# Attention and SwiGLU on one core: high parts of the up weights at 192 modulo 256 bytes, low parts at 64, one order of products for all chunks

## The chip, the cores and the metric

One core of a Trainium2 chip runs the whole program. The metric is the device time of one execution in microseconds, taken as the median of several. Engines are named as the profile names them: PE is TensorE's matmul (PEld its weight load), DVE is VectorE, ACT is ScalarE, POOL is GpSimd, SP is SyncE, whose queue starts most DMAs.

## The reference

Block-causal attention and, on its output, a feed-forward layer with a gate. q, k and v are float32, the three weights float64.

```python
B, H, S, D = 8, 8, 576, 64                     # blocks of 64 positions
scores = q @ k.T / sqrt(D), masked where block_i < block_j
attn_out = softmax(scores) @ v
x = attn_out.transpose(0, 2, 1, 3).reshape(4608, 512)
g = x @ w_gate                                 # 512 x 1536
out = (g * sigmoid(g) * (x @ w_val)) @ w_out   # 1536 x 512
```

## The kernel before

**Products.** PE multiplies in float32r, which keeps fewer bits than float32. So each operand is split into a high part, rounded by ACT, and a low part, the rest, made by DVE; a product of two such operands is three matmuls: high by high, high by low, low by high. A matmul has a standing operand (the weights of the array, 128 columns, loaded ahead of it by PEld while the matmul before still runs) and a moving operand that streams past, here 256 columns of 4 bytes.

**The up weights.** w_gate and w_val are kept in SBUF as high (x = 0) and low (x = 1) tiles, made by `weight`: w_gate's odd chunks of 128 columns in `g_odd0` and `g_odd1`, its even chunks in `g_even0` and `g_even1`, w_val's chunks in `v_all0` and `v_all1` (lines 227 to 230). `w_at(which, x, i)` (line 231) gives chunk i of either matrix and either part. The pool hands out bytes in the order in which the tiles are asked for. In the program as built, before the change, the six tiles start at these bytes of a partition: g_odd0 1984, g_odd1 14272, v_all0 26560, v_all1 51136, g_even0 75712, g_even1 88064. Modulo 256 that is 192 for all of them but g_even1, which stands at 0, because g_even0 was given 16 more elements. Chunks of 512 bytes inside a tile keep the number. x's parts (`xhl`, and the tiles that take their place later) all stand at 0 modulo 256.

**Stages.** (1) Attention for 8 batches, with POOL for maxima and sums over partitions. (2) Between its products stand those of the feed-forward tiles of 256 tokens: `up` (matmuls at L1270, weights standing, x moving), then tanh on ACT and two products on DVE, then the down products (L1381 to L1383). (3) The last 1536 tokens go in three wide tiles of 512, by a scheme with 7 block products in place of 8. There `Pair.product` (L1717) takes w_gate's and w_val's own chunks for the products named 1 to 4, and sums of chunks for 5, 6 and 7, which come by DMA from `mix_d` into a ring of buffers in `sc`. High and low part of the ring's buffers both stand at 64 modulo 256, by an offset of 16 elements (`shifted`). (4) The last stage makes the output of the wide tiles and of the last narrow tiles (`product_of`, L2033). In it w_out's blocks, which by then lie in the places of the up weights, are the *moving* operand, and the hidden values stand; their high and low parts are all at 0 modulo 256.

**The order.** Every piece of work is a task with an engine, a rank, buffers and what it waits for. `in_order` plays the engines through with estimated costs and writes down one order, which is then issued, so the order on each engine is fixed before the kernel runs. The up products of a chunk are one task of 12 matmuls (four blocks d, three matmuls each); for the first two tiles they are four tasks of 3. Each task's list of matmuls is written in `products`:

```python
three = [[(lo, d, 0), (hi, d, 0), (hi, d, 1)] for d in ds]
if which or y:
    three = [[b, c, a] for a, b, c in three]
elif len(ds) > 1:
    three = [[a for a, b, c in three]] + [[b, c] for a, b, c in three]
```

So w_val's chunks and w_gate's odd ones go high, high, low for each d; w_gate's even chunks begin with the four low parts and go on with the eight high ones. `Pair.on_pe` asks for the same of the gate's products 1 and 2 in the wide tiles (`low_first`).

Of the kernel before, what the change touches and what calls it, by code (L numbers as in the profile page):

```python
# [7 lines left out]
F32 = mybir.dt.float32  # L8
F32R = mybir.dt.float32r
# [9 lines left out]
def kernel(  # L19
# [20 lines left out]
    DFF = w_gate.shape[1]  # L40
    P = 128
# [6 lines left out]
    NDC = DM // P  # L48
# [48 lines left out]
    const = ctx.enter_context(tc.tile_pool(name="const", bufs=1))  # L97
# [79 lines left out]
    def add(engine, cost, rank, fn, after=(), bufs=(), port=False, mode="", stage=""):  # L177


        bufs = [*dict.fromkeys([*bufs, *(p for u in bufs for p in getattr(u, "under", ()))])]  # L180
        t = Task(engine, cost, rank, fn, after, bufs, port, mode)
        for a in after:
            if a is not None:
                a.next.append(t)
                t.waits += 1
        for u in bufs:
            u.left += 1
        t.n, t.stage = len(tasks), stage
        tasks.append(t)
        return t  # L190


    def act_us(n, psum=False, more=0.0):
        return (0.05 if psum else 0.093) + n * 0.000833 + more

    def dve_us(n, one=False):
        return 0.07 + n * (0.00052 if one else 0.00104)

    def up_us(n):
        return n * 0.1134 + (0.012 if n < 3 * NDC else 0.0)  # L200
# [24 lines left out]


    half_w, whole_w = [P, NDC, DFF // 2], [P, NDC, DFF]
    g_odd = [const.tile(half_w, F32R, name=f"g_odd{x}") for x in range(2)]
    v_all = [const.tile(whole_w, F32R, name=f"v_all{x}") for x in range(2)]
    g_even = [const.tile([P, NDC * DFF // 2 + 16 * (1 - x)], F32R, name=f"g_even{x}") for x in range(2)]  # L230

    def w_at(which, x, i):

        if which:
            return v_all[x][:, :, i * P : (i + 1) * P]
        if i % 2:
            return g_odd[x][:, :, i // 2 * P : (i // 2 + 1) * P]
        every = g_even[x][:, 0 : NDC * DFF // 2].rearrange("p (c f) -> p c f", c=NDC)
        return every[:, :, i // 2 * P : (i // 2 + 1) * P]
# [987 lines left out]
    def feed_forward(j, t0, w, xs):  # L1227
# [19 lines left out]
        def rank(i):  # L1247
            return (10.0 + (t0 + w * i / NFC) / S) if j > 1 else SIDE[j] + w * i / NFC / S

        def up(i, which, prev):  # L1250

            ps = Buf("gv")
            ts = up_done[0]
            for y in range(2):

                chunk = []
                for ds in [range(NDC)] if j >= WHOLE else [[d] for d in range(NDC)]:

                    def products(ds=ds, y=y):
                        hi, lo = (w_at(which, k, i + y) for k in range(2))  # L1260
                        o = ps[0][:, y * w : (y + 1) * w]
                        three = [[(lo, d, 0), (hi, d, 0), (hi, d, 1)] for d in ds]
                        if which or y:
                            three = [[b, c, a] for a, b, c in three]
                        elif len(ds) > 1:
                            three = [[a for a, b, c in three]] + [[b, c] for a, b, c in three]
                        for n, (part, d, x) in enumerate(sum(three, [])):
                            first = n == 0 and 0 in ds
                            last = n == 3 * len(ds) - 1 and NDC - 1 in ds
                            nc.tensor.matmul(  # L1270
                                o, lhsT=part[:, d], rhs=xs[d][1][x][:, 0:w], start=first, stop=last
                            )

                    ts = add(
                        "PE",
                        up_us(3 * len(ds)),
                        rank(i),
                        products,
                        [ts, *(xs[d][0] for d in ds), w_done[i + y, which]],
                        [ps, *(xs[d][1] for d in ds)],  # L1280
                        stage="up",
                    )
                    ts.prev = prev
                    ts.chunk, ts.ds = chunk, ds
                    ts.even = len(ds) > 1 and not (which or y)
                    prev = ts if j >= FINE else None
                last_use.setdefault((which, i + y), []).append(ts)
            chain["up"] = up_done[0] = ts
            return ps, ts

        for i in range(0, NFC, 2):
# [37 lines left out]
            a = add("ACT", act_us(n, True), E, tanh, [tg], [pg, t])  # L1329
            a = add("DVE", dve_us(n), E, silu2, [a], [pg, t])  # L1330
            a = add("DVE", dve_us(n), E, gated, [a, tv], [pv, t, hh] if put_off else [pv, t])
            if put_off:
                u, x = divmod(j - normal + 2 * DEFER, 2)
# [12 lines left out]
            a = add("ACT", act_us(n, to is pv), E, high, [a], [to, hh])  # L1346
            a = add("DVE", dve_us(n), E, low, [a], [to, hh], to is t)
# [126 lines left out]
    def wide_tiles(mixed):  # L1474
# [189 lines left out]
        def on_pe(*args, after=(), **more):  # L1664
            line[0] = add("PE", *args[:3], [*after, line[0]], args[3], **more)
            return line[0]
# [17 lines left out]
        class Pair:  # L1684
# [42 lines left out]
            def on_pe(self, names):  # L1727
                bufs, after = [*dict.fromkeys(self.ps[SPOT[n][0]] for n in names)], []
                for name in names:
                    bufs += [self.xs[XN[name], c] for c in range(2)]  # L1730
                    after += [self.ready[XN[name], c] for c in range(2)]
                    if name in self.ring:
                        bufs.append(self.ring[name])
                        after.append(self.loads[name])
                    if name == "3":
                        after.append(kept[self.which, self.i])

                def products():
                    self.product(names, "1" in names and not self.which)

                return on_pe(up_us(6 * len(names)), self.rank, products, bufs, after=after, stage="up")

# [533 lines left out]
    with tc.manual_schedule():  # L2276
        done, shared = set(), None
        in_turn = mybir.DependencyInfo(mybir.DependencyClass.Sync, mybir.DependencyReason.DATA)
        for t in order:
# [14 lines left out]
            ds = list(t.ds)  # L2294
# [34 lines left out]
```

## Time and profile before

| what | value |
|---|---|
| median of 3 runs (lowest, highest) | 1134.91 us (1133.3, 1136.73) |
| profiled execution | 1136.55 us |
| its span, first to last instruction | 1134.7 us |
| PE, DVE, ACT, POOL busy | 98%, 85%, 54%, 27% |
| matmuls in the trace | 9612 |
| mean granted clock of TensorE | 0.997 of full speed |

The share of busy time of an engine says how much of the span it had an instruction in work. A matmul is pipelined: the next one starts long before the last one is through, so a row's time of one matmul (some 276 to 285 ns here) is its way through the array and not what it costs. What it costs is the distance from its start to the next start. For a row of several matmuls that is the start of the next row less its own start, divided by their number.

### The profile page before, as it was taken

What the parts mean: (1) busy time and instruction counts of PE and PEld (TensorE: products, weight loads), DVE (VectorE), ACT (ScalarE), POOL (GpSimd) and SP (SyncE); (2) the same over time, 40 slices, a digit from 0 to 9 for tenths busy, and PEclk for the clock granted to TensorE, in tenths of its full rate; (3) what the DMA queues carried; (4) which work ended last, traced back from release to release, by engine and by line L of the source; (5) the groups of instructions that cost most, each with busy time, mean ns of one, the idle gap of its engine ahead of it and who ended that gap; (6) DMA issues with size and microseconds to landing.
All of it is one profiled execution on the core that took longest, in us unless ns stands there. A gap on an engine that the chain in (4) does not pass through costs nothing. (4 is left out here: it accounts for less than half of the span.)

```text
span 1134.7 us, 25286 instructions
## 1 busy us (share of the span) xinstructions
PE 1114.1 (98%) x9612; PEld 1031.0 (91%) x9612; DVE 959.5 (85%) x1772; ACT 610.6 (54%) x1115; POOL 309.4 (27%) x141
## 2 busy tenths in 40 slices
PE   7999999999999999999999999999999999999998
PEld 6777888898899999999999899999999999999998
DVE  5998888677979999999998977767698887998884
ACT  6988877556555546665665555554242222454441
POOL 3113111053544264455435553553000000000000
PEclk9999999999999999999999999999999999999999
DMA  7877666576656767887877654337788976554442
GB/s 205 209 210 202 188 194 218 148 203 195 160 150 211 182 184 202 232 216 192 214 202 199 166 145 119 92 119 220 207 272 242 294 235 216 166 158 146 126 149 75
DMA packets 332617, 211.66 MB, mean 187 GB/s; under 512 B 194192, under 2 KB 290976, under 8 KB 332496
## 3 DMA queue, kind: packets, MB, share of 16 engines
q1 hardware_dynamic: 331264, 209.39, 64.3%
q8 instruction: 75, 1.23, 0.5%
q10 hardware_dynamic: 1232, 0.66, 0.2%
q14 instruction: 46, 0.38, 0.1%
HBM read 157.29 MB, written 52.69 MB: 185 GB/s over the span
## 5 line engine op out<-in xcount | busy, mean ns | idle before, releaser
L1028 POOL PARTITION_ALL_REDUCE mx<-mx x48 | 173.2, 3640 | 204.7 <-DVE mx L823 78.1
L1270 PE MATMUL gv<-xhl,v_all 128*128 128x256 f32 x1728 | 218.7, 279 | 0.6 <-DVE hhl L1317 0.6
L1270 PEld LDWEIGHTS gv<-xhl,v_all 128*128 128x128 f32 x1728 | 208.0, 188 | 4.3 <-issue 1.0
L827 POOL PARTITION_ALL_REDUCE mx<-mx x80 | 134.5, 1718 | 268.6 <-DVE wo L1127 46.0
L853 DVE TENSOR_TENSOR sc<-sc,mx 128x640 f32<-128x640 f32 (+5 forms) x168 | 127.0, 805 | 13.1 <-POOL mx L827 12.8
L1270 PE MATMUL gv<-xhl,g_even 128*128 128x256 f32 x864 | 121.1, 285 | 3.8 <-DVE t L1310 3.4
L857 ACT ACTIVATE sc<-sc 128x1024 f32<-128x1024 f32 (+3 forms) x104 | 105.0, 1029 | 33.6 <-DVE sc L853 32.8
L1270 PEld LDWEIGHTS gv<-xhl,g_even 128*128 128x128 f32 x864 | 108.9, 188 | 11.8 <-DVE t L1310 4.9
L1270 PE MATMUL gv<-xhl,g_odd 128*128 128x256 f32 x864 | 113.5, 278 | 0.0
L1270 PEld LDWEIGHTS gv<-xhl,g_odd 128*128 128x128 f32 x864 | 105.5, 188 | 2.0 <-issue 1.7
L776 ACT ACTIVATE sc<-at 128x1024 f32<-128x1024 f32 (+3 forms) x96 | 78.5, 843 | 2.7 <-DVE mx L821 1.4
L1307 ACT ACTIVATE t<-gv 128x512 f32<-128x512 f32 x72 | 43.4, 602 | 57.0 <-PE gv L1270 57.0
L750 PE MATMUL at<-parts,qk 64*128 64x320 f32 (+5 forms) x864 | 73.7, 310 | 0.0
L939 PE MATMUL at<-sc,v 128*64 128x192 f32 (+1 forms) x960 | 70.7, 302 | 0.3 <-issue 0.3
L939 PEld LDWEIGHTS at<-sc,v 128*64 128x64 f32 x960 | 61.3, 137 | 10.4 <-issue 1.8
L1768 DVE TENSOR_TENSOR sc<-sc,at 128x512 f32<-128x512 f32 x92 | 56.5, 615 | 16.5 <-ACT sc L1773 8.1
L750 PEld LDWEIGHTS at<-parts,qk 64*128 64x128 f32 x864 | 62.7, 185 | 8.4 <-issue 1.4
L1310 DVE SCALAR_TENSOR_TENSOR t<-t,gv 128x512 f32<-128x512 f32 x72 | 48.9, 680 | 23.3 <-ACT t L1307 22.9
L1381 PE MATMUL po<-wo,hhl 128*128 128x512 f32 x156 | 63.7, 409 | 0.0
L823 DVE TENSOR_TENSOR mx<-mx,sc 128x384 f32<-128x384 f32 (+2 forms) x108 | 59.0, 549 | 2.8 <-ACT sc L857 1.5
L1382 PE MATMUL po<-wo,hhl 128*128 128x512 f32 x156 | 61.3, 393 | 0.0
L1383 PE MATMUL po<-wo,hhl 128*128 128x512 f32 x156 | 60.9, 390 | 0.0
(408 smaller groups left out, 2327.4 us busy)
## 6 DMA issues: line engine op xcount, KB each, us to landing
wo<-wo_d SPq DMA_DIRECT2D x80, 512.0 KB
sc<-mix_d SPq DMA_DIRECT2D x72, 256.0 KB
h_d<-hhl SPq DMA_DIRECT2D x60, 256.0 KB
mix_d<-wo SPq DMA_DIRECT2D x48, 256.0 KB
v<-in_v_dram SPq DMA_DIRECT2D x64, 128.0 KB
mx<-h_d SPq DMA_DIRECT2D x30, 256.0 KB
parts<-h_d SPq DMA_DIRECT2D x30, 256.0 KB
qk<-in_q_dram SPq DMA_DIRECT2D x104, 72.0 KB
```

The costliest lines, as they stand in the source:

```text
L750: nc.tensor.matmul(ps[0][:, x, o : o + w], lhsT=part(1, kl)[own(x), c * P : (c + 1) * P], rhs=part(0, ql)[own(x), qs : qs + w], start=n == ...
L776: nc.scalar.mul(sc[0][:, :, o0 : o0 + gw], ps[0][:, :, 0:gw], SCALE)
L823: nc.vector.tensor_tensor(into, prev, of(c), op)
L827: nc.gpsimd.partition_all_reduce(m, m, channels=P, reduce_op=bass_isa.ReduceOp.max)
L853: nc.vector.tensor_tensor(piece(c), scores_of(c), m, ALU.subtract)
L857: nc.scalar.activation(x, x, AF.Exp)
L939: nc.tensor.matmul(third(k)[own(x), q0 - s0 :], lhsT=vt[0][:, c, own(x)], rhs=sc[0][:, x, place[c] + q0 - first[c] : place[c] + s1 - first ...
L1028: nc.gpsimd.partition_all_reduce(m, m, channels=P, reduce_op=bass_isa.ReduceOp.add)
L1270: nc.tensor.matmul(o, lhsT=part[:, d], rhs=xs[d][1][x][:, 0:w], start=first, stop=last)
L1381: nc.tensor.matmul(po, lhsT=hi, rhs=whi, start=i + y == 0, stop=False)
L1382: nc.tensor.matmul(po, lhsT=hi, rhs=wlo, start=False, stop=False)
L1383: nc.tensor.matmul(po, lhsT=lo, rhs=whi, start=False, stop=i + y == NFC - 1)
```

## The change

The six tiles are asked for in another order, with fillers between: g_odd0, v_all0, g_even0, then 128 bytes, then g_odd1, v_all1, g_even1, then 192 bytes. In the program as built they start at 1984, 14272, 38848 (all 192 modulo 256) and 51264, 63552, 88128 (all 64). Every later tile of the pool lies 256 bytes further on. And w_gate's even chunks, in the narrow and in the wide tiles, go high, high, low for each d as the others do. As the last stage reads w_out's blocks from the same places, its moving operand now steps between 192 and 64 too, except in the product named 3, of which both parts lie in g_even0.

```diff
     half_w, whole_w = [P, NDC, DFF // 2], [P, NDC, DFF]
-    g_odd = [const.tile(half_w, F32R, name=f"g_odd{x}") for x in range(2)]
-    v_all = [const.tile(whole_w, F32R, name=f"v_all{x}") for x in range(2)]
-    g_even = [const.tile([P, NDC * DFF // 2 + 16 * (1 - x)], F32R, name=f"g_even{x}") for x in range(2)]
+
+    shapes = {"g_odd": half_w, "v_all": whole_w, "g_even": [P, NDC * DFF // 2]}
+    parts_of_w = {name: [] for name in shapes}
+    for x, gap in enumerate((32, 48)):
+        for name, shape in shapes.items():
+            parts_of_w[name].append(const.tile(shape, F32R, name=f"{name}{x}"))
+        const.tile([P, gap], F32, name=f"gap{x}")
+    g_odd, v_all, g_even = parts_of_w.values()
...
                         three = [[(lo, d, 0), (hi, d, 0), (hi, d, 1)] for d in ds]
-                        if which or y:
+                        if which or y or len(ds) > 1:
                             three = [[b, c, a] for a, b, c in three]
-                        elif len(ds) > 1:
-                            three = [[a for a, b, c in three]] + [[b, c] for a, b, c in three]
...
                 def products():
-                    self.product(names, "1" in names and not self.which)
+                    self.product(names)
```

On PE, a piece of w_gate's even chunks behind a down stretch, in the middle of the kernel. Before (g_even0 holds the high parts, g_even1 the low ones; xhl0_0 is the high part of x's first block, xhl0_1 its low part):

```order
L1383 MATMUL po0_0_259<-wo1_0_2141,hhl0_1_111 128x512
L1270 MATMUL gv1_0_189<-xhl0_0_89,g_even1_73 128x256
L1270 MATMUL gv1_0_189<-xhl1_0_91,g_even1_73 128x256
L1270 MATMUL gv1_0_189<-xhl2_0_93,g_even1_73 128x256
L1270 MATMUL gv1_0_189<-xhl3_0_95,g_even1_73 128x256
L1270 MATMUL gv1_0_189<-xhl0_0_89,g_even0_72 128x256
L1270 MATMUL gv1_0_189<-xhl0_1_90,g_even0_72 128x256
L1270 MATMUL gv1_0_189<-xhl1_0_91,g_even0_72 128x256
L1270 MATMUL gv1_0_189<-xhl1_1_92,g_even0_72 128x256
L1270 MATMUL gv1_0_189<-xhl2_0_93,g_even0_72 128x256
```

With the change, the same place:

```order
L1386 MATMUL po0_0_261<-wo1_0_2143,hhl0_1_113 128x512
L1273 MATMUL gv1_0_191<-xhl0_0_91,g_even0_70 128x256
L1273 MATMUL gv1_0_191<-xhl0_1_92,g_even0_70 128x256
L1273 MATMUL gv1_0_191<-xhl0_0_91,g_even1_74 128x256
L1273 MATMUL gv1_0_191<-xhl1_0_93,g_even0_70 128x256
L1273 MATMUL gv1_0_191<-xhl1_1_94,g_even0_70 128x256
L1273 MATMUL gv1_0_191<-xhl1_0_93,g_even1_74 128x256
L1273 MATMUL gv1_0_191<-xhl2_0_95,g_even0_70 128x256
L1273 MATMUL gv1_0_191<-xhl2_1_96,g_even0_70 128x256
L1273 MATMUL gv1_0_191<-xhl2_0_95,g_even1_74 128x256
```

The twelve matmuls are the same; the low parts have moved from the front, where four of them followed each other, to the third place of each triple.

On PE, the gate's products 1 and 2 of a wide tile, with other tiles (qk) in the place of xhl. Before:

```order
L1717 MATMUL at0_0_9075<-qk1_0_8400,g_even1_73 128x256 x2
L1717 MATMUL at0_1_9076<-qk1_0_8400,g_even1_73 128x256
L1717 MATMUL at0_1_9076<-qk0_0_8650,g_even1_73 128x256
L1717 MATMUL at0_0_9075<-qk1_0_8400,g_even0_72 128x256 x4
L1717 MATMUL at0_1_9076<-qk1_0_8400,g_even0_72 128x256 x2
L1717 MATMUL at0_1_9076<-qk0_0_8650,g_even0_72 128x256 x2
```

With the change:

```order
L1720 MATMUL at0_0_9077<-qk1_0_8402,g_even0_70 128x256 x2
L1720 MATMUL at0_0_9077<-qk1_0_8402,g_even1_74 128x256
L1720 MATMUL at0_0_9077<-qk1_0_8402,g_even0_70 128x256 x2
L1720 MATMUL at0_0_9077<-qk1_0_8402,g_even1_74 128x256
L1720 MATMUL at0_1_9078<-qk1_0_8402,g_even0_70 128x256 x2
L1720 MATMUL at0_1_9078<-qk1_0_8402,g_even1_74 128x256
L1720 MATMUL at0_1_9078<-qk0_0_8652,g_even0_70 128x256 x2
L1720 MATMUL at0_1_9078<-qk0_0_8652,g_even1_74 128x256
```

Here too the four low parts have moved from the front to the third place of each triple. On DVE, ACT, POOL and SP every instruction keeps its place.

## Rows read from the trace of the kernel before

**Rows 1.** the page's part 1, all engines: busy us (share) x instructions

```profile
PE 1114.1 (98%) x9612; PEld 1031.0 (91%) x9612; DVE 959.5 (85%) x1772; ACT 610.6 (54%) x1115; POOL 309.4 (27%) x141
```

**Rows 2.** waits of PE, 600 to 850 us: total us, times, longest

```profile
PE gv L1270 <- DVE t L1310: 2.6, 4, 0.9
...
PE po L1717 <- DMA sc<-mix_d: 0.5, 2, 0.3
```

**Rows 3.** busy time from 850 us on: stretch, length, engines, clock, DMA

```profile
850.00:1129.50 279.50, 279.50 (x2420) 279.21 (x2419) 238.58 (x494) 100.03 (x204) 0.00 (x0) 1.00 0.58 182
```

**Rows 4.** timeline of PE, 784 to 793 us: start, us, engine line operation

```profile
784.40 1.65 PE L1270 MATMUL gv<-xhl,g_even 128*128 128x256 f32 x12
...
787.25 2.88 PE L1270 MATMUL gv<-xhl,v_all 128*128 128x256 f32 x24
789.97 1.55 PE L1270 MATMUL gv<-xhl,g_even 128*128 128x256 f32 x12
791.36 1.52 PE L1270 MATMUL gv<-xhl,g_odd 128*128 128x256 f32 x12
792.72 2.88 PE L1270 MATMUL gv<-xhl,v_all 128*128 128x256 f32 x24
```

**Rows 5.** timeline of PE, 609 to 616 us

```profile
609.47 1.68 PE L1270 MATMUL gv<-xhl,g_even 128*128 128x256 f32 x12
...
612.40 2.99 PE L1270 MATMUL gv<-xhl,v_all 128*128 128x256 f32 x24
615.23 0.40 PE L1381 MATMUL po<-wo,hhl 128*128 128x512 f32 x1
```

**Rows 6.** chain that ended last, in order of time, last stage: start, us

```profile
981.84 4.95 PE at L2033 x42
...
1103.47 2.47 PE at L2033 x21
...
1108.42 2.38 PE at L2033 x21
```

**Rows 7.** timeline of PE around 1107 us

```profile
1106.84 0.91 PE L2033 MATMUL po<-v_all,xu 128*128 128x256 f32 x6
```

**Rows 8.** groups by line and shape, PE: count, busy us, mean ns, idle before

```profile
L1270 PE MATMUL gv<-xhl,v_all 128*128 128x256 f32 x1728 | 218.7, 279 | 0.6 <-DVE hhl L1317 0.6
L1270 PE MATMUL gv<-xhl,g_even 128*128 128x256 f32 x864 | 121.1, 285 | 3.8 <-DVE t L1310 3.4 <-DVE xhl L392 0.2
L1270 PE MATMUL gv<-xhl,g_odd 128*128 128x256 f32 x864 | 113.5, 278 | 0.0
...
L1717 PE MATMUL at<-wo,sc 128*128 128x256 f32 x144 | 18.3, 276 | 0.0
```

**Rows 9.** timeline of PE, 822 to 836 us (sc is the ring)

```profile
822.78 0.84 PE L1717 MATMUL gv<-parts,sc 128*128 128x256 f32 x6
...
825.87 0.87 PE L1717 MATMUL po<-parts,v_all 128*128 128x256 f32 x6
...
833.66 1.57 PE L1717 MATMUL gv<-qk,v_all 128*128 128x256 f32 x12
835.08 0.84 PE L1717 MATMUL gv<-parts,sc 128*128 128x256 f32 x6
```

**Rows 10.** timeline of PE, 809 to 810 us

```profile
809.12 0.84 PE L1717 MATMUL at<-qk,sc 128*128 128x256 f32 x6
809.80 0.84 PE L1717 MATMUL at<-parts,g_odd 128*128 128x256 f32 x6
```

**Rows 11.** timeline of PE, first and last rows of counted kinds

```profile
28.44 0.96 PE L1270 MATMUL gv<-xhl,g_even 128*128 128x256 f32 x3
...
31.94 0.62 PE L1270 MATMUL gv<-xhl,g_even 128*128 128x256 f32 x3
...
66.56 0.98 PE L1270 MATMUL gv<-xhl,g_even 128*128 128x256 f32 x6
...
972.13 1.55 PE L1717 MATMUL at<-xhl,g_even 128*128 128x256 f32 x12
```

## The prediction

> **What bounds the kernel now.** I read the engines' busy time first, then what TensorE waits for, then the chain of waits, and last the timeline of TensorE alone. PE is busy 98% of the span, the next engine 85% [rows 1]; between 600 and 850 us, where it waits most, the waits that the trace ascribes are 2.6 us on DVE's t and half a microsecond on a DMA [rows 2]. From 850 us to the end of the products PE has no idle time at all, with the clock granted in full (1.00 of 2.4 GHz) [rows 3]. So the time is the number of matmuls times the distance from one start to the next, and I looked for a part of that distance which is not work.
>
> It is there. The piece of v_all from 787.25 to the next start at 789.97 has 24 matmuls of 256 columns: 2.72 us, **113.3 ns** each [rows 4]. The same piece of the same tile at 612.40 takes until 615.23: 2.83 us, **117.9 ns** [rows 5]. Neither waits, the shapes and the clock are equal. The chain shows the same in the last stage, with weights as the moving operand: 21 matmuls in 2.47 us for most of it, 2.38 us from 1108.42 on, after one piece of six at 1106.84 that lasts 0.91 us [rows 6, 7]. I call these the short and the long pitch. A stretch keeps the pitch it has: at 609.47 it starts long and stays long through three tiles [rows 5], at 784.40 it is short after one piece and stays so up to 789.97 and beyond [rows 4]. Nothing of the work done differs, so the difference must lie in how the weight load beside a matmul and the matmul's own reads fall together. Where the tiles lie is told by the built program; with it, the trace shows three things:
> - Weights at 0 modulo 256 (only g_even's low part) cost more than either: the 12 of g_even at 789.97 take 1.39 us, the 12 of g_odd behind them 1.36 us [rows 4]. The group's mean is 285 ns against 278 and 279 [rows 8]. Behind such a run the pitch is mostly short; at 609.47 it is not [rows 5].
> - Going from weights at 192 to weights at 64 (the ring in sc) while the pitch is long makes it short: v_all at 833.66 has 12 in 1.42 us to the next start, 118 ns each, and the ring's six right behind it at 835.08 last 0.84 us, where six at the long pitch last 0.87; so too at 822.78. Going back from 64 to 192 while long does not: v_all at 825.87 stays at 0.87 us [rows 9].
> - While the pitch is short, both steps are free: 64 at 809.12, 192 at 809.80, all 0.84 us [rows 10].
>
> **The change part by part.** Every triple is now high, high, low, and the low part lies 128 bytes off the high one modulo 256. So each third load is a step from 192 to 64, and by the second and third observations it ends a long pitch and costs a short one nothing. No instruction is added, and on the other four engines the order is the same; only PE's matmuls inside 86 pieces change places. The tiles behind move by 256 bytes, that is not at all modulo 256.
> - Up products and the first products of the wide tiles, with weights in g or v other than g_even's low runs: between the row at 31.94 and the one at 833.66, 1339 of the distances are long, mean 117.8 ns [rows 9, 11]. 1339 x 4.5 ns = **6.0 us** off.
> - The runs of low parts at 0 modulo 256: 287 distances from the row at 66.56 to the one at 972.13, mean 119.5 ns [rows 11]. 287 x 6.2 ns = **1.8 us** off. The cover for this is the reset that these runs gave; the step from 192 to 64 has to take it over.
> - Last stage, weights moving: from 981.84 to the flip at 1107, 1054 long distances [rows 6, 7]. 1054 x 4.5 ns = **4.7 us** off, if here too the alternation ends the long pitch. This the trace does not show: its moving operand never alternates. Bounds: 4.7 us off (2.38 us for 21 throughout), or as much as 2 us added (119.5 ns, the dearest pitch in the trace, in place of 117.8, 1054 x 1.7 ns). I take the gain, since what counts in the other stages is the distance between the two addresses read at a time, and this alternates here as well.
> - What stays: the first triple of a stretch can still be long. There are 113 stretches, from the row at 28.44 to the one at 784.40 [rows 4, 11]; three distances x 4.5 ns x 113 = **1.5 us** back. Zero if stretches start short; so 0 to 1.5.
> - What is late next: between 600 and 850 us PE waits on DVE and on the ring's loads [rows 2]. About 570 of the long and low distances lie there, so 2.7 us of the gain arise there. A wait on DVE work that itself follows PE moves along, one on a DMA that started by its own clock does not; I take **1.0 us** back, between 0 and 2.7.
> - The order in g_even's pieces needs the low part of x at the second matmul instead of the sixth, 0.45 us earlier. PE's waits on xhl are 0.2 us in all [rows 8], so this costs 0 to 0.2 us; I take 0. The 128-byte moves of the DMA targets change no size and no packet; 0.
>
> Sum: 6.0 + 1.8 + 4.7 - 1.5 - 1.0 = 10.0 us off. The profiled execution took 1136.55 us (span 1134.7 and 1.85 us around it), 1.6 us above the median of 1134.91. 1136.55 - 10.0 = 1126.55; carried to the median, **1124.9 us**.
>
> **The rivals.**
> - *Only the stages with weights standing gain.* For it: no row shows a moving operand that steps by 128 bytes; and more than a thousand distances hold the long pitch there, whatever tile stands in the array [rows 6]. Then the last stage keeps its 4.7 us: 1134.91 - 5.3 = 1129.6 us; with up to 2 us added there, 1131.6.
> - *The long pitch loses its way out* (the other side). The change removes the low runs at 0, behind which most stretches turn short. If one low load at 64 between high ones at 192 is too little to turn the pitch (in the rows that turn, six loads at 64 follow each other), or the step back from 64 to 192 restores it, as at 825.87 [rows 9], then a stretch that enters long stays long. At worst all 4124 distances of these stages are long: 18.6 us instead of the 7.8 us of now, 1145.7 us. It decides from about 1730 long distances (7.8 us / 4.5 ns). Against it: the ring's six at 835.08 take the 0.84 us of a wholly short six, so the turn comes with the first loads, and in the short pitch the step back is free [rows 9, 10].
> - *Addresses do not matter at all.* Then the pitch is set by something that the change leaves alone (the delay with which a stretch begins), 192 and 64 do nothing, and the 1.8 us of the low runs go or move to the stretches that they no longer turn: 1134.9 us, within a few us. Against it stand the ring's rows [rows 9], for it that they are two. The Trainium skill has this as a rule: "SBUF — State Buffer", section "Who interferes with whom", gives PE two independent read ports, one for the moving operand and one for weight loads, and says that "PE and ACT never wait on anyone"; by it the first two terms and the third would be zero. The trace does not agree: one tile, one shape and one clock have two pitches [rows 4, 5].
>
> **How the numbers follow.** The forecast has 0.52: the turn in the stages with standing weights seems likely (about 0.8), its likeness in the last stage a little over even. Only the first stages: 0.27. No way out: 0.11. No effect of addresses: 0.10. A measurement of this kernel tells about 0.3%, 3.4 us, from no change. The forecast lies below that, and so do four fifths of the first rival (0.22): faster 0.74. Its remainder (0.05) and the third rival are the same: 0.15. Slower: 0.11. The forecast's own range is 1121.5 (all 12.5 us, and a run 1 us under the median) to 1128; that of the text takes in the first and third rivals, **1121.5 to 1137**, and leaves out the second.
>
> **What the changed profile would show.** Right: the mean of g_even's group falls from 285 ns to that of the other two, and those fall toward 276, the value of a matmul at the short pitch; v_all's pieces of 24 take 2.72 us to the next start wherever they stand, the long ones of 2.83 us gone; in the last stage 21 matmuls take 2.38 us from the first row of the chain on, so that it is 4.7 us shorter from its first product to its last. First rival: this last one stays at 2.47. Second: pieces of 24 at 2.83 us everywhere before 800 us. Third: long and short stretches in about today's numbers. The forecast is wrong as well if PE's waits between 600 and 850 us grow by the whole gain.

## The result and the profile after

The changed kernel takes 1140.62 us (median of 20 runs, 1137.39 to 1147.33), the kernel before, beside it on the same chips, 1135.49 us (20 runs, 1132.19 to 1139.03). The ratio is **1.0052, with a 95% interval from 1.0038 to 1.0066**: about half a per cent slower. The forecast was 1124.9 us with a range up to 1137.0; the time lies above it, on the side of the second rival (the long pitch loses its way out). The profiled execution took 1138.44 us, 2.2 us under its median, with a span of 1136.5 us.

The page's part 1 of the changed kernel (busy us, share of the span, instructions; against [rows 1]):

```profile
PE 1116.8 (98%) x9612; PEld 1033.7 (91%) x9612; DVE 955.2 (84%) x1772; ACT 611.9 (54%) x1115; POOL 310.1 (27%) x141
```

As many matmuls, 2.7 us more of PE's time. Where it lies is told by the groups by line and shape (count, busy us, mean ns of one, idle before; against [rows 8]):

```profile
L1273 PE MATMUL gv<-xhl,v_all 128*128 128x256 f32 x1728 | 220.9, 280 | 0.6 <-DVE hhl L1320 0.6
L1273 PE MATMUL gv<-xhl,g_even 128*128 128x256 f32 x864 | 121.4, 285 | 2.7 <-DVE t L1313 2.4 <-DVE xhl L397 0.3
L1273 PE MATMUL gv<-xhl,g_odd 128*128 128x256 f32 x864 | 114.7, 280 | 0.0
```

g_even's mean stays at 285 ns, where the forecast had it fall; v_all's goes from 279 to 280 and g_odd's from 278 to 280. The timeline of PE between 643 and 668 us (start us, us, then the instruction) shows what stretches do now:

```profile
643.48 1.53 PE L1273 MATMUL gv<-xhl,g_even 128*128 128x256 f32 x12
644.85 1.52 PE L1273 MATMUL gv<-xhl,g_odd 128*128 128x256 f32 x12
646.21 2.88 PE L1273 MATMUL gv<-xhl,v_all 128*128 128x256 f32 x24
648.93 1.52 PE L1273 MATMUL gv<-xhl,g_even 128*128 128x256 f32 x12
...
658.31 1.06 PE L755 MATMUL at<-parts,qk 64*128 64x320 f32 x12
659.30 1.69 PE L1273 MATMUL gv<-xhl,g_even 128*128 128x256 f32 x12
660.83 1.59 PE L1273 MATMUL gv<-xhl,g_odd 128*128 128x256 f32 x12
662.26 3.01 PE L1273 MATMUL gv<-xhl,v_all 128*128 128x256 f32 x24
665.20 1.97 PE L755 MATMUL at<-parts,qk 64*128 64x448 f32 x24
```

The stretch from 643.48, which follows a down stretch, is short throughout: 1.37, 1.36 and 2.72 us to the next start. The one from 659.30, which follows attention's products (L755), never leaves the long pitch: 1.43 us for g_odd's twelve (119 ns each), 2.94 us for v_all's 24, although every third load is one at 64 behind one at 192.

The wide tiles show that a run of loads at 64 is no sure way out either. The ring's pieces (sc), all at 64, behind a long piece of w_val:

```profile
813.83 1.59 PE L1720 MATMUL gv<-qk,v_all 128*128 128x256 f32 x12
815.26 0.87 PE L1720 MATMUL gv<-parts,sc 128*128 128x256 f32 x6
815.96 0.87 PE L1720 MATMUL po<-mx,sc 128*128 128x256 f32 x6
816.67 0.87 PE L1720 MATMUL po<-qk,sc 128*128 128x256 f32 x6
```

In the kernel before, the same tiles turned short at the ring's first six [rows 9]. Here all 18 stay long (0.70 and 0.71 us to the next start), and so do the 18 from 820.23 on. The load in front of them stands at 64 now, no longer at 192, so the ring no longer begins with a step. In the second execution of the changed kernel the same two rings stay long.

In the last stage nothing is won. The chain of waits in order of time (start, us; against [rows 6]) has about the 2.47 us of the long pitch to the end, 118 ns each for 18 and for 24 matmuls too:

```profile
1104.38 2.47 PE at L2036 x21
...
1124.22 2.47 PE at L2036 x21
1126.70 2.12 PE gv L2036 x18
1128.82 2.84 PE po L2036 x24
```

PE's waits between 600 and 850 us (total us, times, longest) fell by 0.9 us on DVE's t [rows 2]; those on the ring's loads (mix_d) come to 0.8 us, against 0.9 before (0.4 of at and 0.5 of po):

```profile
PE gv L1273 <- DVE t L1313: 1.7, 4, 0.6
PE at L1720 <- DMA sc<-mix_d: 0.8, 2, 0.6
```

Put together from the start times of all 256-column matmuls: what the distances lie above 113.3 ns, in us (in brackets how many are over 115 ns; those over 136 ns are waits and are left out), of two executions of each kernel:

| stage | before | before again | after | after again |
|---|---|---|---|---|
| up (L1270; L1273) | 7.1 (1496) | 6.9 (1462) | 10.7 (1911) | 10.8 (1937) |
| wide tiles, own chunks | 0.8 (140) | 0.8 (140) | 0.6 (109) | 0.5 (85) |
| wide tiles, ring | 0.1 (23) | 0.2 (34) | 0.4 (86) | 0.4 (78) |
| last stage | 4.7 (1054) | 2.4 (528) | 5.1 (983) | 5.1 (969) |

The up stage pays 3.7 us more, the ring 0.2. In the last stage the kernel before does not always pay 4.7 us. Its second execution has 2.4; two pieces from that one's chain, at the same addresses:

```profile
1058.67 2.38 PE at L2033 x21
...
1078.24 2.47 PE at L2033 x21
```

That stage begins long, turns short at 992 us and long at 1076, each time at two distances of 198 to 443 ns, where PE was held up for a moment. In the first execution places of that kind at 990 and 1077 us leave the pitch long, and one at 1106.84 turns it short [rows 7]. Five profiles in which its moving operand steps nowhere, or only in the products that read g_even (two of the kernel itself, and E2, E3 and E7 below), have 4.7, 2.4, 3.6, 0.4 and 0.4 us, a mean of 2.3; after the change it is 5.1 each time, so 2.8 us more on average. The distances that are waits, in the wide tiles' products, total 3.1 and 3.3 us over 113.3 ns before, 1.8 and 1.6 after: 1.5 us less. 3.7 + 0.2 + 2.8 - 0.2 - 1.5 = 5.0 us, against 5.13 between the medians. That the two lie so close is partly luck, since the last stage's 2.3 us is a mean over other kernels too. In the four profiles themselves these terms come to 3.8 us (1.6 us more in the last stage), and the spans differ by 2.5 us on average: the distances of the up stage that are waits and left out of the table are 0.7 us less, the matmuls of attention and the fillers between 0.4 us less. Both profiled executions of the kernel before are above its median (1136.55 and 1137.0 us), both of the changed kernel below its own (1138.44 and 1140.07 us).

### The profile page after: what moved, and what is told of

Its sections match the earlier page's. It is cut to its first block, busy times and chain, and to the rows that moved or that the text cites. A ratio compares the mean times of both kernels' runs of the same rounds, so it can differ in the third digit from the quotient of the medians.

```text
span 1136.5 us, 25286 instructions
## 1 busy us (share of the span) xinstructions
PE 1116.8 (98%) x9612; PEld 1033.7 (91%) x9612; DVE 955.2 (84%) x1772; ACT 611.9 (54%) x1115; POOL 310.1 (27%) x141
## 5 line engine op out<-in xcount | busy, mean ns | idle before, releaser
L1273 PE MATMUL gv<-xhl,v_all 128*128 128x256 f32 x1728 | 220.9, 280 | 0.6 <-DVE hhl L1320 0.6
L1273 PEld LDWEIGHTS gv<-xhl,v_all 128*128 128x128 f32 x1728 | 209.9, 188 | 4.5 <-issue 1.0
L1273 PE MATMUL gv<-xhl,g_even 128*128 128x256 f32 x864 | 121.4, 285 | 2.7 <-DVE t L1313 2.4
L1273 PEld LDWEIGHTS gv<-xhl,g_even 128*128 128x128 f32 x864 | 109.1, 188 | 10.5 <-DVE t L1313 3.6
L1273 PE MATMUL gv<-xhl,g_odd 128*128 128x256 f32 x864 | 114.7, 280 | 0.0
L1273 PEld LDWEIGHTS gv<-xhl,g_odd 128*128 128x128 f32 x864 | 106.6, 188 | 2.0 <-issue 1.7
L755 PE MATMUL at<-parts,qk 64*128 64x320 f32 (+5 forms) x864 | 73.6, 310 | 0.0
L1771 DVE TENSOR_TENSOR sc<-sc,at 128x512 f32<-128x512 f32 x92 | 56.7, 616 | 16.8 <-ACT sc L1776 8.5
L755 PEld LDWEIGHTS at<-parts,qk 64*128 64x128 f32 x864 | 62.7, 185 | 8.4 <-issue 1.4
```

What stands on the lines that cost most here:

```text
L755: nc.tensor.matmul(ps[0][:, x, o : o + w], lhsT=part(1, kl)[own(x), c * P : (c + 1) * P], rhs=part(0, ql)[own(x), qs : qs + w], start=n == ...
L1273: nc.tensor.matmul(o, lhsT=part[:, d], rhs=xs[d][1][x][:, 0:w], start=first, stop=last)
```

## The experiments

The two kernels ran once more as they were, for a second profile of each, and gave 1137.0 us (before) and 1140.07 us (after), and the second and fourth columns above.

> The kernel before once more. Theory A: stretches begin at the same pitch as in its first profile where they begin behind the same products; the last stage may come out wholly short (0.4 us over 113.3 ns each, as where g_even's low part stood at 192) or wholly long (4.7 us), by the phase in which it starts. Rival E: 4.7 us again, as the order and the addresses are the same.

> The changed kernel once more, to see how much of its spread (1137 to 1147 us) the pitch explains. Theory A: time over the first profiled execution goes with the sum of long distances, in stretches that begin behind attention's products and in the last stage; where the run takes 5 us more, the distances of the 256-column matmuls sum to some 5 us more. Rival E (something else, waits or DMA, spreads it): the distances sum to the same within 1 us.

The kernel before: the up stage is as in the first profile (6.9 and 7.1 us), and the last stage came out neither wholly short nor wholly long. The changed kernel: its distances over 113.3 ns sum to 16.8 us in both executions, though the second took 1.6 us more; it is 2.2 us behind already at 250 us. So what spreads these two is not the pitch, as rival E had it. Six of the 20 executions of the result took 1144.6 to 1147.3 us; none of these was profiled, so what makes them slow stays open.

**E1, the layout alone.** The tiles of the change, the old order of the products: low parts first in w_gate's even chunks, now at 64.

```diff
-    g_odd = [const.tile(half_w, F32R, name=f"g_odd{x}") for x in range(2)]
...
+    for x, gap in enumerate((32, 48)):
+        for name, shape in shapes.items():
+            parts_of_w[name].append(const.tile(shape, F32R, name=f"{name}{x}"))
+        const.tile([P, gap], F32, name=f"gap{x}")
```

> High parts at 192, low parts at 64, but w_gate's even chunks begin with their four low parts as before. Theory A (the way out): a stretch keeps the pitch it starts with, a single low load at another offset is too little to change it, several in a row are enough. Then the four low loads at 64 in a row turn the pitch as the ring's did, at no extra cost of their own: the median is 2 to 6 us under the kernel before, 1130 to 1134 us, and pieces of v_all behind an even piece have the short distance of 113.3 ns. Rival B (the layout): alternation of 192 and 64 in the standing weights is itself what costs; then it is like the change, 1138 to 1143 us, with pieces of v_all at 118 ns and above.

Measured: 1137.86 us against 1134.57, 1.0038 (1.0018 to 1.0058), above the range of theory A and just below that of rival B. Up 8.3 us, last stage 5.1. The layout alone costs, 2.8 us of it in the last stage, and the timeline of PE shows why the up stage is dearer by only 1.3 us:

```profile
643.29 1.58 PE L1275 MATMUL gv<-xhl,g_even 128*128 128x256 f32 x12
644.71 1.59 PE L1275 MATMUL gv<-xhl,g_odd 128*128 128x256 f32 x12
646.13 3.01 PE L1275 MATMUL gv<-xhl,v_all 128*128 128x256 f32 x24
648.98 1.52 PE L1275 MATMUL gv<-xhl,g_even 128*128 128x256 f32 x12
...
659.18 1.64 PE L1275 MATMUL gv<-xhl,g_even 128*128 128x256 f32 x12
660.66 1.52 PE L1275 MATMUL gv<-xhl,g_odd 128*128 128x256 f32 x12
662.02 2.88 PE L1275 MATMUL gv<-xhl,v_all 128*128 128x256 f32 x24
664.83 1.97 PE L755 MATMUL at<-parts,qk 64*128 64x448 f32 x24
```

These are the two stretches shown of the changed kernel, and both have swapped their pitch. Behind attention's products four low loads in a row turn the pitch (g_odd 1.36 us, v_all 2.81 to the L755 behind it, against 1.43 and 2.94). Behind a down stretch they do not (1.42, 1.42, 2.85), where high, high, low does.

**E2, the order alone.** The layout of before, w_gate's even chunks high, high, low.

```diff
-                        if which or y:
+                        if which or y or len(ds) > 1:
...
-                    self.product(names, "1" in names and not self.which)
+                    self.product(names)
```

> The addresses of before, but w_gate's even chunks go high, high, low. Theory A: the runs of four loads at 0 are gone, and with them most turns to the short pitch; each low load at 0 still costs its 6 ns. The median is 3 to 12 us over the kernel before, 1138 to 1147 us, the number of long distances at L1270 rises from 1300 to 2000 or more. Rival B (the layout is what costs): as before, 1134 to 1137 us.

Measured: 1142.43 us against 1134.57, 1.0076 (1.0056 to 1.0095). Up 14.1 us, 2969 of 3272 distances long; wide tiles 2.6, ring 1.4, last stage 3.6. With the low runs at 0 gone and nothing at 64 in their place, almost nothing in the up stage turns the pitch. In the wide tiles the single low loads at 0 even turn short to long: the piece of w_gate's even chunks at 845.23 begins at 114 and 113 ns and goes on at 122, 117 and 118, and the ring's 18 loads at 64 behind it stay long; in the tiles that follow this repeats. The terms sum to 11.5 us over the kernel before, the medians differ by 7.9; the profiled execution was itself 3.0 us above its median.

**E3, the low part of the even chunks at 192.** Order of before, all six tiles at 192.

```diff
-    g_even = [const.tile([P, NDC * DFF // 2 + 16 * (1 - x)], F32R, name=f"g_even{x}") for x in range(2)]
+    g_even = [const.tile([P, NDC * DFF // 2 + 16 * x], F32R, name=f"g_even{x}") for x in range(2)]
```

> The order of before, with the low part of w_gate's even chunks at 192 modulo 256 like all others (no 16 elements between). Theory A: four low loads at the same offset as the rest turn nothing, so a stretch that starts long stays long: 3 to 10 us over the kernel before, 1138 to 1146 us. Rival C (it is the order, four different weights in a row, and not their address that turns the pitch): the turns stay, the 1.8 us of the dear low loads go, 1133 to 1134.5 us.

Measured: 1137.88 us against 1134.57, 1.0037 (1.0023 to 1.0051). Up 13.9 us, 3132 of 3271 long, though the low parts come first as in the kernel before. The only edit moves g_even1's start down by 64 bytes, so the low run turns the pitch by its address; that the order matters as well is what E2 shows. The terms sum to 4.4 us over the kernel before (the last stage was short here), the medians differ by 3.3. Two stretches of its timeline, both long (1.42, 1.41 and 2.83; 1.52 and 1.41):

```profile
647.19 1.58 PE L1270 MATMUL gv<-xhl,g_even 128*128 128x256 f32 x12
648.61 1.58 PE L1270 MATMUL gv<-xhl,g_odd 128*128 128x256 f32 x12
650.02 2.99 PE L1270 MATMUL gv<-xhl,v_all 128*128 128x256 f32 x24
652.85 1.58 PE L1270 MATMUL gv<-xhl,g_even 128*128 128x256 f32 x12
...
662.46 1.68 PE L1270 MATMUL gv<-xhl,g_even 128*128 128x256 f32 x12
663.98 1.57 PE L1270 MATMUL gv<-xhl,g_odd 128*128 128x256 f32 x12
665.39 2.99 PE L1270 MATMUL gv<-xhl,v_all 128*128 128x256 f32 x24
```

Its last stage, on the other hand, was short (0.4 us), from the chain:

```profile
1124.19 2.38 PE at L2033 x21
```

E1 and E3 issue the same instructions in the same order and differ in addresses alone: 8.3 and 13.9 us. That the addresses do not matter, the third rival, is out. By the rule of the Trainium skill that it named ("SBUF — State Buffer", section "Who interferes with whom": two independent read ports, PE never waits) they would not matter, and these two runs do not agree with that. Whether it is a read port at which the matmuls are held up no run shows.

**E4, a nudge.** In the last stage of the kernel before, a bf16 matmul of 8 to 200 columns ahead of 20 of the products, into a place of PSUM that the product then overwrites. It adds work whose result is thrown away.

```diff
-                    o = ps[m].view()[:, x * w : (x + 1) * w]
+                    o = flat = ps[m].view()[:, x * w : (x + 1) * w]
...
+                        if starts_bank and name in "17":
+                            kicks.append(0)
+                            cols = (8, 16, 24, 32, 48, 64, 96, 128, 160, 200)[(len(kicks) - 1) * 3 % 10]
+                            bf = mybir.dt.bfloat16
+                            nc.tensor.matmul(flat[:, 0:cols], lhsT=ones.bitcast(bf), rhs=ident.bitcast(bf)[:, 0:cols], start=True, stop=True)
```

> The kernel before, with one more small matmul (bfloat16, 8 to 200 columns, overwritten by the product that follows) ahead of 20 of the last stage's products, to see which delays turn the pitch there. Theory A in its wider form (the pitch is the phase between a matmul's reads and the weight load beside it): some delays turn long to short and others short to long, at a weight address that never changes; the last stage then shows stretches of both pitches, split by the size of the delay. Rival D (the pitch follows from the operands' addresses alone): the last stage keeps 117.8 ns between the added matmuls whatever their size.

Measured: one run, 1138.28 us. The timeline around 1010 us (L2039 is the added matmul):

```profile
1009.88 0.52 PE L2040 MATMUL po<-v_all,sr 128*128 128x256 f32 x3
1010.23 0.19 PE L2039 MATMUL at<-ident,ones 128*128 128x24 bf16 x1
1010.27 0.59 PE L2040 MATMUL at<-g_odd,xhl 128*128 128x256 f32 x3
1010.70 0.50 PE L2040 MATMUL at<-g_odd,qk 128*128 128x256 f32 x3
1011.04 0.50 PE L2040 MATMUL at<-v_all,qk 128*128 128x256 f32 x3
1011.38 0.20 PE L2039 MATMUL at<-ident,ones 128*128 128x64 bf16 x1
...
1012.20 0.50 PE L2040 MATMUL at<-g_even,qk 128*128 128x256 f32 x3
```

Three matmuls take 0.35 us up to 1010.23 and 0.34 from 1010.70 on, at the same addresses as in the kernel before: the pitch behaves like a phase, which one small matmul can turn. It costs 0.04 us itself and about 0.09 in the row behind it (0.43 against 0.34), 0.13 together. Widths of 24, 16, 8 and 32 turned long to short here, 48, 8 and 32 turned short to long, 64 left it short, and behind 96 to 200 it was always long. So rival D is out.

**E6, the nudge at 64 columns alone**, ahead of five products; otherwise the kernel before. The edit is that of E4 with these lines:

```diff
-                        if starts_bank and name in "17":
+                        if starts_bank and name in "1" and s == 0:
...
-                            cols = (8, 16, 24, 32, 48, 64, 96, 128, 160, 200)[(len(kicks) - 1) * 3 % 10]
+                            cols = 64
```

> The kernel before, with one added bfloat16 matmul of 64 columns (overwritten by the product behind it) ahead of the last stage's first product and of four later ones. In the survey such a matmul cost 0.125 us and left a short pitch short; from a long one it was not seen. Theory A in its wider form: the last stage is short for most of its length, 4.7 us over 113.3 ns each become 0.3 to 1.5 us, 0.6 us is spent on the added matmuls; 1131 to 1133 us. Rival D (the operands' addresses fix the pitch): 4.7 us stay and 0.6 us come on top, 1135 to 1136 us.

Measured: 1135.07 us against 1135.25, 1.0002 (0.9987 to 1.0016). The last stage's excess is 0.95 us, 3.8 less than in [rows 6], but the median did not move. Five nudges cost 0.6 us, and against a mean of 2.3 us, not 4.7, only 0.7 us are to be had, less than the interval tells. At 1036.36, where the stage was long, the nudge of 64 columns turned it short, which E4 had not seen.

**E5, the changed kernel with low parts first behind attention's products only.** The two orders each where it turned the pitch.

```diff
+    entry = {"attention": False, "stage": ""}
...
+                        if entry["attention"] and len(ds) > 1:
+                            three = [[c for a, b, c in three]] + [[a, b] for a, b, c in three]
...
+            if t.engine == "PE":
+                entry["attention"], entry["stage"] = entry["stage"] not in ("up", "down"), t.stage
```

> The changed kernel, with the low parts first in an up piece that directly follows attention's products, and high, high, low elsewhere. Theory F (how a stretch starts decides: behind down products a piece of high, high, low turns short, behind attention's products one with four low parts first): the up distances over 113.3 ns fall from 10.7 us to 3 to 4.5 us, the last stage keeps 5.1 us; 1131 to 1135 us at the median. Rival B (the layout is what costs): no better than with the low parts first everywhere, 1137 to 1139 us.

Measured: 1138.16 us against 1135.25, 1.0031 (1.0012 to 1.005), which misses theory F's time. Up 4.9 us, less than half of the changed kernel's and 2 under the kernel before; the last stage 5.6 us, long. Two of its stretches, both behind attention's products and with the same order, one that turns (g_odd 1.36) and one that does not (1.43):

```profile
660.23 1.64 PE L1277 MATMUL gv<-xhl,g_even 128*128 128x256 f32 x12
661.70 1.52 PE L1277 MATMUL gv<-xhl,g_odd 128*128 128x256 f32 x12
663.06 2.88 PE L1277 MATMUL gv<-xhl,v_all 128*128 128x256 f32 x24
...
667.77 1.68 PE L1277 MATMUL gv<-xhl,g_even 128*128 128x256 f32 x12
669.29 1.59 PE L1277 MATMUL gv<-xhl,g_odd 128*128 128x256 f32 x12
670.72 1.47 PE L1277 MATMUL gv<-xhl,v_all 128*128 128x256 f32 x11
```

The stages sum to about 1 us more than before (-2.1 up, +3.3 last stage, -0.3 in the wide tiles), the medians differ by 2.9; the rest is not explained.

The up stage by how a stretch begins (excess in us, long of all distances where counted), stretches that begin with w_gate's even chunks. The last column holds, beside those behind attention's products, a few behind filler matmuls or wide tiles:

| kernel | low part at, order | behind a down stretch | behind attention's products |
|---|---|---|---|
| before | 0, four low first | 0.8 (152 of 895) | 2.9 (617 of 1649) |
| E2 | 0, high high low | 3.8 (814) | 6.9 (1438) |
| E3 | 192, four low first | 3.9 (882) | 6.8 (1542) |
| after | 64, high high low | 0.4 (69) | 8.3 (1484) |
| E1 | 64, four low first | 4.3 (785) | 1.8 (331) |
| E5 | 64, each where it turned | 0.4 | 3.1 (561) |

Counted by the first piece of 12 of such stretches, in the first profile of each: behind down products 18 of 19 end it short before, 18 after, 1 in E1; behind attention's products 16 of 26 before, 2 after, 22 in E1 and 21 in E5. So the rule is one of most cases, not of all. In the kernel before, the run at 0 turns the pitch only where a stretch begins or behind a wait: the five such pieces that directly follow a long piece stay long.

**E7, only the even chunks' low part at 64.** All else stays at 192, so the last stage's moving operand alternates only in the products that read g_even; order as in E5, for w_gate's even chunks. The tiles' line is shown against the kernel before:

```diff
-    g_even = [const.tile([P, NDC * DFF // 2 + 16 * (1 - x)], F32R, name=f"g_even{x}") for x in range(2)]
+    g_even = [const.tile([P, NDC * DFF // 2 + 32 + 16 * x], F32R, name=f"g_even{x}") for x in range(2)]
...
+                        if entry["attention"] and len(ds) > 1 and not (which or y):
+                            three = [[c for a, b, c in three]] + [[a, b] for a, b, c in three]
```

> Only g_even's low part at 64 (all other parts, high and low, at 192 as before), so the last stage's moving operand does not alternate; w_gate's even chunks go high, high, low, but with their four low parts first where the piece directly follows attention's products. Theory F plus theory G (in the last stage it is the alternation of the moving operand that takes the steady short pitch away): the last stage again shows long runs of one pitch, 100 distances and more, short ones among them, and 0.4 to 4.7 us over 113.3 ns; the up distances sum to 5 to 6 us over, against 7.1 before; the median is 0.5 to 3 us under the kernel before, 1132 to 1135 us. Rival B (any alternation of 192 and 64 costs more than it turns): up at 8 us or more, 1136 to 1139 us.

Measured: 1135.05 us against 1136.26, 0.9986 (0.9969 to 1.0003). Up 4.8 us, last stage 0.4: with the rest of w_out's parts at one address it can be short, and was. The interval just takes in no change, so a gain is not shown.

**E8, E7 with the nudge of 64 columns ahead of three products of the last stage.**

```diff
+                        if starts_bank and name in "1" and s == 0 and j % 2 == 0:
```

> As the run before it, with the added matmul of 64 columns ahead of three products of the last stage (its first, and the first of every second tile). Theory A in its wider form: 0.4 us are spent on them, the last stage is short for most of its length in every execution, 0.4 to 1.5 us over; 1131 to 1133.5 us. Rival D: the last stage as without them, 0.4 us slower than the run before.

Measured: 1132.6 us against 1136.26, **0.9973 (0.9956 to 0.9989)**: faster than the kernel before by about 0.3%. Up 5.1 us. The last stage has 2.0 us, more than theory A had: its chain is long from 1017 to 1037 us, where the second nudge (at 1036.99) turns it, again from 1067 to 1074 us, and from 1104.84 us to the end.

```profile
1012.40 2.38 PE at L2042 x21
...
1017.37 2.47 PE at L2042 x21
...
1037.20 2.48 PE at L2042 x21
...
1042.06 2.38 PE at L2042 x21
...
1099.84 2.38 PE at L2042 x21
...
1104.84 2.47 PE at L2042 x21
```

So the nudge turns the pitch but does not hold it, and how much of the gain is its own the runs do not tell: the intervals of E7 and E8 overlap, and E7, with the slower median, has the lower sum in the last stage (0.4 us).

## Why the prediction was wrong

- **"The time is the number of matmuls times the distance from one start to the next."** Right in kind: the excess over 113.3 ns and the waits, added up above, have the sign and about the size of the slowdown. But the busy time of [rows 3] hides that PE is held up now and then: the last stage of that same trace has five distances of 173 to 254 ns, and at such places the pitch can turn.
- **"Each third load is a step from 192 to 64 ... it ends a long pitch and costs a short one nothing."** This is the step that failed. A single load at 64 between high ones turns the pitch behind a down stretch (excess 0.8 to 0.4 us where w_gate's even chunks begin, and 1.39 to 0.15 us where w_val's do). Behind attention's products it does not: 2.9 became 8.3 us. The distances at 597.44 in the changed kernel are 119, 112, 118, 115 and 119 ns and then long: the steps disturb the pitch and it falls back, as the second rival had it. There mostly a run of low loads is needed (E1 1.8 us). The rows that this was read from, the ring's six loads at 64, were a run; the second rival said so, and I held their first loads to have done it. Nor was the run enough by itself: in the changed kernel the ring's 18 at 815.26 stay long, behind a load that stands at 64 as well.
- **"1.8 us off" for the runs at 0.** The saving is there where a piece is short: g_even's twelve at 643.48 take 1.37 us against 1.39 at 789.97 [rows 4]. But these runs were the way out of the long pitch: without them and without 64 (E2) the up stage pays 14.1 instead of 7 us. I had named this cover, and priced its loss only in the rival.
- **A long distance costs 4.5 ns, before and after.** Too little for the new layout: where high, high, low stays long, g_odd's twelve at 660.83 take 119 ns each, 5.9 ns over the short pitch.
- **"4.7 us off" in the last stage.** Both halves failed. The alternation does not end the long pitch there; with it the stage is mostly long: 5.1, 5.1, 5.1 and 5.6 us in four profiles with that layout. And 4.7 us was one sample; five profiles without it average 2.3, two of them 0.4. The flip in [rows 7] was a sign that this stage's pitch is turned by moments at which PE is held up, and I carried it as a fixed size.
- **"1.5 us back" for starts, "1.0 us back" for waits.** The cost of starts is real (most stretches behind a down stretch begin with one or two long distances). With no gain there was nothing to give back in waits; those in the wide tiles' products fell by 1.5 us instead, and why no run shows.
- **The rivals.** The second, at 0.11, names the mechanism, in part of the stages: 1911 long distances in the up stage alone, over the 1730 from which I had it decide, not the 4124 of its worst case. The first is out (the standing stages lose too), the third by E1 and E3.

Open: why the start addresses give two phases at all (that "the difference must lie in how the weight load beside a matmul and the matmul's own reads fall together" was argued and no run shows it); whether 256 bytes is the right unit, since every move was tried at one distance only; why most stretches behind down products answer to one order and most behind attention's products to the other; why the changed kernel's times spread over 10 us where the kernel before spreads over 7; and E5's 2 us. In the first 250 us PE's place in the program moves by some -2.5 to +4.3 us from one execution to another, whatever the kernel, so a single profile can't settle a term of 2 us.

## What to carry to other kernels

When one instruction of one shape has two durations in a trace, measure first how much the share of each varies between executions of the same kernel, and only then price the dear one: here half of a 4.7 us term was chance. A pattern that seems to reset such a state (a run of loads at another address) must be taken as it stands in the rows, its length and what ran before it included; a piece of it, or the same piece behind other work, can do the opposite. And before the dear part of a mixture is removed, ask whether it is what makes the rest cheap, and try it: E2 showed it in one experiment.

## What the runs showed that I had not expected

- The same addresses in the same order hold either of two distances, 113.3 or about 118 ns, for hundreds of matmuls, and a matmul of 24 columns between them turns one into the other for 0.13 us (E4).
- With the moving operand stepping between 192 and 64, the last stage has no steady short pitch: 970 to 983 of its 1254 distances are long in the profiles of the changed kernel and of E1 (1078 in E5), with short ones singly or three together between them, and its 5.1 us over 113.3 ns are dearer than the stage of [rows 6] with more long ones (1054, 4.7 us).
- Without that stepping the last stage holds one pitch for up to 806 distances (E2). Where it changes for long, a nudge or a distance of 129 ns or more stands at the change, in all the profiles without the stepping.
- Which order turns the pitch depends on the work in front: E1 and the changed kernel differ only in the order inside w_gate's even chunks, and the excess behind down stretches (4.3 and 0.4 us) and behind attention's products (1.8 and 8.3 us) goes opposite ways.
